# A fused attention and two-layer feed-forward kernel: block sums by accumulating transfers, separate rings for the weight parts, a new order of products and copies

## The chip, the cores and the metric

One core of one Trainium2 chip. The metric is device time in microseconds of the whole kernel; the lower the better. The profile shows one execution on that core. PE is TensorE (matmuls), DVE is VectorE, ACT is ScalarE, POOL is GpSimd, SP is SyncE, whose queue issues most loads. Each engine runs its own instructions in one fixed order.

## The reference

Retention (attention without softmax, with a decay instead) on 4 x 8 heads of 576 tokens of 64, then two feed-forward layers on the 2304 x 512 result:

```
scores = 0.125 * q @ k.T ;  ret = scores * Dmat        # Dmat[i,j] = gamma_h ** (i-j), 0 above the diagonal
x  = (ret @ v), heads side by side                     # 2304 x 512
h  = x @ w_in                                          # 512 -> 2048
g  = (a0 + a1*h + a2*h^2 + a3*h^3) / (1 + |b0|*|h| + |b1|*h^2 + 1e-6)
x  = g @ w_out                                         # 2048 -> 512
g  = s * max(x @ w_in2, 0)^2 + b ;  out = g @ w_out2   # second layer, 2048 wide too
```

All of it is fp32.

## The kernel before

Every product is made of three fp32r matmuls (`three`, line 360): an operand is kept as a rounded high part and a low part (the rest), and high x low, low x high, high x high are added in PSUM. A high part is cast on ACT, a low part is a subtraction on POOL or DVE. Weights come from DRAM as 1 MB tiles `raw` of 64-bit words, one per column tile `kf` (0 to 15 first layer, 16 to 31 second), each with a part of w_in and one of w_out. `w_round` (line 115) rounds them in three DVE steps and one ACT step, `w_split` (line 130) writes high and low parts into one of five slots `w0` to `w4`. `next_load` (line 95) issues the next raw load. Two raw tiles have permanent buffers; tiles 2, 5, 8, ... have a third one that is there only in some stages (`extra_raw`, lines 89 to 97).

*Retention* (lines 151 to 301) runs over 16 pairs of heads; loads go out five pairs ahead on SP. PE, DVE, ACT and POOL orders are pinned to the program order (`keep_in_program_order`). One step of the first three weight cuts stands in each pair from the third on. Line 283 issues raw loads in pairs 3 and 7; the one in pair 7 is tile 2, and the first steps on tile 2 stand in pair 7 as well.

*First layer* (`emit_in`, `rational`, `out1`, lines 385 to 443): 80 units, each a column tile by a block of 512 tokens (or 256, tokens 2048 to 2303). A unit is 12 matmuls into a bank `h`, a chain of 13 ACT, DVE and POOL instructions (`rational`), and 12 matmuls of w_out into four banks `o`, which DVE adds to `acc`. The out-products lag by two or three units. Except where pinned, a planner in the compiler sets the order of instructions within ACT, DVE, POOL and SP from the program order and its own estimate of readiness.

*Second layer.* 16 quads (`quad`, line 666), eight for each pair of 512-token blocks (a pass). A quad takes two column tiles, k = 16 + 2q and k + 1, and makes its four 512 x 128 results with seven half-size products (`PRODUCTS`, line 602, a Winograd scheme) instead of eight. For that it needs sums of token blocks, "1" to "4" (`x_sum`, line 512: four DVE instructions of 1024 elements for each pass, in place in `acc`, then `x_split`), and sums of weights S1 to S4 (`s_sums`, `s_split`). The first quad of each pass works with eight plain products while these are made. `fill` (line 672) sets out-products of the quad before (`out2`; at quad 0 those of the last units) between the products. Results leave a quad by `relu2` (line 612): four ACT instructions and a DVE subtraction. The 256 tail tokens are done in the first pass (`tail_in`, line 656). In pass one every quad rounds and splits the next quad's weights (`cut_first`, `cut_second`), keeps the split parts in DRAM (`w_keep`) and prepares the second pass's token blocks (`x_keep`); the second pass fetches them again (`w_fetch`, `s_fetch`, `x_fetch`), all by POOL's queue.

In a quad the order of the matmuls is product 1, 5, two fills, 6, two fills, 2, fills, 7, fills, 3, two fills, tail, 4, tail. ACT copies the bank of product 1 into hB ahead of product 6:

```
756  nc.scalar.copy(hB, hA)
760  nc.scalar.copy(g5, hG)
763  product(q, 6, hB, False)
790  relu2(("q", q, 1, 0), hB, 512, True)      # last result of a quad, from the same bank hB
```

Of the kernel before, what the change touches and what calls it, by code (L numbers as in the profile page):

```python
# [27 lines left out]
W_BUFS = 5  # L28
W_EARLY = 4
WTMP_BUFS = 1  # L30
RAW_BUFS = 2
# [11 lines left out]
def retention_ffn_kernel(ctx, tc, a, b, s2, b2, w, qkv, maskv, gdec, out):  # L43
# [14 lines left out]
    stg = ctx.enter_context(tc.tile_pool(name="stg", bufs=RAW_BUFS))  # L58
# [23 lines left out]
    w_slots = {}  # L82
    w_both = {}
# [5 lines left out]
    raw_extra = [None]  # L89

    def extra_raw(kf):

        return kf % 3 == 2 and kf < NF

    def next_load(eng=nc.sync, pin=free):
        if w_ahead and not (extra_raw(w_ahead[0]) and raw_extra[0] is None):
            w_load(w_ahead.pop(0), eng, pin)

    def w_slot_tiles(pool, slots):
        for i in slots:  # L100
            w_both[i] = pool.tile([P, 2, 2, NC, P], F32R, name=f"w{i}")
            w_slots[i] = [w_both[i][:, x] for x in range(2)]

    w_slot_tiles(wpool, range(W_EARLY))

    def w_load(kf, eng, pin):
        pool = raw_extra[0] if extra_raw(kf) else stg
        w_raw[kf] = t = pool.tile([P, 2 * DM], I64, tag="raw", name=f"raw{kf}")
        pin(eng.dma_start(out=t, in_=w[kf]))
# [5 lines left out]
    def w_round(kf, pinned=False):  # L115
# [4 lines left out]
        pin = tc.keep_in_program_order if kf < W_FIRST + RAW_BUFS + 1 else free  # L120
# [9 lines left out]
    def w_split(kf, pinned=False):  # L130
        rest = tc.keep_in_program_order if pinned else free
        f = w_words(kf)[1].bitcast(F32)
        wh, wl = w_slots[kf % W_BUFS]
        whf, wlf = (x.rearrange("p w c f -> p (w c f)") for x in (wh, wl))
        for which in range(2):
            w_t[kf, which] = (wh[:, which], wl[:, which])
        rest(nc.scalar.copy(whf, f))  # L137
        nc.gpsimd.tensor_tensor(out=wlf, in0=f, in1=f32(whf), op=ALU.subtract)  # L138
# [12 lines left out]
    def retention(actx):  # L151
# [152 lines left out]
    def ffn(fctx):  # L304
# [11 lines left out]

        rawctx = ExitStack()
        raw_extra[0] = rawctx.enter_context(tc.tile_pool(name="rawx", bufs=1))
        next_load()
# [3 lines left out]
        def raw_to_g():  # L323
            rawctx.close()
            gpx = fctx.enter_context(tc.tile_pool(name="gpx", bufs=1))
            g_free.extend((gpx, i) for i in range(G_BUFS[1] - G_BUFS[0]))
# [16 lines left out]
        def g_tiles(u, n):  # L343
# [5 lines left out]
            pool, i = g_used[u] = g_free.pop(0)  # L349
            whole = [pool.tile([P, 512], F32R, tag=f"{x}{i}", name=f"{x}{number(u)}") for x in ("gh", "gl")]  # L350
# [34 lines left out]
        def emit_in(u):  # L385
# [7 lines left out]
            hps[u] = ps  # L393

        def rational(u):
# [14 lines left out]
            nc.vector.scalar_tensor_tensor(out=tt, in0=r, scalar=-2.0, in1=tt, op0=ALU.add, op1=ALU.mult)  # L410
# [115 lines left out]
        def x_keep(i, c):  # L526
# [9 lines left out]
            if c == 1:  # L536
                for x in NEXT.get(key, ()):
# [19 lines left out]
        def s_sums(q):  # L557
# [5 lines left out]
            nc.vector.tensor_tensor(out=s3, in0=a["11"], in1=a["21"], op=ALU.subtract)  # L563
            nc.vector.tensor_tensor(out=s2, in0=s1, in1=a["11"], op=ALU.subtract)
            nc.vector.tensor_tensor(out=s4, in0=a["12"], in1=s2, op=ALU.subtract)
# [13 lines left out]
        def w_keep(kf):  # L579
            w_spill[kf] = spill.tile([P, 2, 2, NC, P], F32, name=f"ws{kf}")  # L580
            nc.gpsimd.dma_start(out=w_spill[kf], in_=f32(w_both[kf % W_BUFS]))

        def w_fetch(kf):
            nc.gpsimd.dma_start(out=w_both[kf % W_BUFS], in_=w_spill[kf - NF])
            for which in range(2):
                w_t[kf, which] = tuple(x[:, which] for x in w_slots[kf % W_BUFS])

        def s_fetch(q):
            t = stg.tile([P, 2, 2, 512], F32R, tag="raw", name=f"sf{q}")
# [66 lines left out]
        def tail_in(q, i, tag):  # L656
# [4 lines left out]
            for c in range(NC):  # L661
                for x in three(ps, (wh[:, c, :], wl[:, c, :]), (xh[:, c, r], xl[:, c, r]), c == 0, c == NC - 1):
                    pe(x)
            relu2(("q", q, i, 2), ps, n, True)

        def quad(q, fills):
# [42 lines left out]
            def cut_second():  # L709
# [3 lines left out]
                if rounds:  # L713
                    next(rounds[1], None)
                    t = s_sums(q + 1)
                    del w_raw[k + 2]
                    next_load()
                    s_split(q + 1, t)

            if q % (NQ // 2) == 0:  # L720
                fill(4)

                for (i, j), tag, key in zip(((0, 0), (0, 1), (1, 1), (1, 0)), ("hA", "hG", "hB", "hT"), ("1", "3", "2", None)):
# [7 lines left out]
                    if key and first:  # L731
# [182 lines left out]
```

## Time and profile before

| | us |
|---|---|
| median of 3 runs (lowest, highest) | 919.59 (917.74, 922.48) |
| the profiled execution | 917.18 |
| span of the profiled execution | 915.4 |
| mean granted clock of TensorE, share of full speed | 0.983 |

The retention stage ends at about 87 us, the first layer's last out-products at about 520, quad 1 starts at 540, the second pass at about 733, and the last matmul ends at 911. "Idle before" in a row is time in which the engine did nothing just before an instruction, and what ended it. A wait on PE is lost time where PE is the busiest engine; a wait elsewhere matters only through what stands behind it.

### The profile page before, as it was taken

How to read it: one execution, taken by the hardware profiler on the slowest of the kernel's cores; microseconds unless marked ns; L12 is line 12 of the kernel's file. 1: busy time of each engine (PE TensorE's matmuls, PEld its weight loads, DVE VectorE, ACT ScalarE, POOL GpSimd, SP SyncE). 2: the span in 40 equal slices, each digit the busy share in tenths (PEclk: the TensorE clock that was granted, in tenths of full speed). 3: DMA queues.
4: the chain of work that ended last, by engine and by line, in shares of the span. 5: the costliest groups of instructions: out<-in, count | busy, mean ns of one | idle time of the engine just before them, and what ended most of it. 6: DMA issues, size and time to landing. Idle time of an engine off the chain costs nothing.

```text
span 915.4 us, 12746 instructions
## 1 busy us (share of the span) xinstructions
PE 856.1 (94%) x4812; PEld 719.7 (79%) x4812; DVE 627.5 (69%) x923; ACT 602.2 (66%) x1001; POOL 405.5 (44%) x328
## 2 busy tenths in 40 slices
PE   6979999899999799999995869999999999999998
PEld 6869788688888688888883758877778888888886
DVE  4856885997877878768969872877766542444445
ACT  1323997887967778678877468667786556554453
POOL 3855563665764655556679533334433300000000
PEclk9989999999999999999998989999999999999999
DMA  8991210111111100101220633566665964444312
GB/s 331 391 330 38 90 47 1 46 47 47 47 47 47 46 16 32 47 1 47 92 92 18 234 116 113 219 243 226 257 229 197 312 227 150 184 179 155 137 47 93
DMA packets 30030, 119.38 MB, mean 130 GB/s; under 512 B 3600, under 2 KB 4112, under 8 KB 20880
## 3 DMA queue, kind: packets, MB, share of 16 engines
q1 hardware_dynamic: 19168, 65.08, 20.0%
q0 software_dynamic: 10800, 53.48, 15.8%
q8 instruction: 38, 0.62, 0.3%
q14 instruction: 24, 0.20, 0.1%
HBM read 83.42 MB, written 35.13 MB: 130 GB/s over the span
## 4 chain that ended last, share of the span: by engine, by line
PE 48%; DVE 16%; DMA 11%; issue 9%; ACT 8%; POOL 7%; SPq 0%; POOLq 0%; ACTq 0%; DVEq 0%
PE p L363 15%; PE o L363 10%; PE h L363 8%; DMA raw<-in_w_dram 8%; PE hB L363 5%; POOL w L138 4%; PE hA L363 3%; PE hG L363 3%; DVE raw L127 2%; DVE wm L124 2%; DVE h L409 2%; DVE tt L408 2%; DVE acc L425 2%; ACT wm L121 1%; DVE tt L410 1%
## 5 line engine op out<-in xcount | busy, mean ns | idle before, releaser
L363 PE MATMUL p<-w,gh 128*128 128x512 f32 x576 | 189.5, 389 | 0.0
L363 PE MATMUL h<-xh,w 128*128 128x512 f32 (+1 forms) x640 | 185.4, 372 | 0.0
L363 PE MATMUL o<-gh,w 128*128 128x512 f32 (+1 forms) x640 | 184.2, 373 | 0.0
L401 POOL TENSOR_TENSOR tq<-tq,ta 128x512 f32<-128x512 f32 (+1 forms) x80 | 103.5, 1295 | 100.7 <-ACT tq L400 98.8
L363 PEld LDWEIGHTS h<-xh,w 128*128 128x128 f32 x640 | 117.9, 191 | 20.8
L363 PEld LDWEIGHTS o<-gh,w 128*128 128x128 f32 x640 | 117.7, 191 | 20.4
L363 PE MATMUL h<-xl,w 128*128 128x512 f32 (+1 forms) x320 | 120.0, 375 | 12.3 <-DVE tt L410 12.2
L363 PE MATMUL o<-gl,w 128*128 128x512 f32 (+1 forms) x320 | 119.6, 375 | 12.5 <-POOL gl L413 9.4
L363 PEld LDWEIGHTS p<-w,gh 128*128 128x128 f32 x576 | 108.1, 188 | 22.4
L651 DVE TENSOR_TENSOR acc<-acc,p 128x512 f32<-128x512 f32 x126 | 85.9, 684 | 57.6 <-PE p L363 57.0
L413 POOL TENSOR_TENSOR gl<-tt,gh 128x512 fp32r<-128x512 f32 (+1 forms) x80 | 102.4, 1284 | 45.5 <-ACT gh L412 37.8
L363 PE MATMUL p<-w,gl 128*128 128x512 f32 x288 | 112.1, 389 | 0.0
L138 POOL TENSOR_TENSOR w<-raw,w 128x1024 fp32r<-128x1024 f32 x32 | 81.2, 2544 | 63.6 <-ACT w L137 63.4
L363 PEld LDWEIGHTS o<-gl,w 128*128 128x128 f32 x320 | 60.9, 191 | 25.8 <-POOL gl L413 10.7
L363 PEld LDWEIGHTS h<-xl,w 128*128 128x128 f32 x320 | 61.1, 191 | 25.0 <-DVE tt L410 14.7
L403 DVE TENSOR_TENSOR tt<-tt,h 128x512 f32<-128x512 f32 (+1 forms) x80 | 50.3, 629 | 34.0 <-ACT tt L402 33.6
L408 DVE SCALAR_TENSOR_TENSOR tt<-tt,aneg,h 128x512 f32<-128x512 f32 (+1 forms) x80 | 55.1, 688 | 23.4 <-ACT h L407 23.2
L400 ACT ACTIVATE tq<-ta,babs 128x512 f32<-128x512 f32 (+1 forms) x80 | 61.9, 776 | 4.8 <-DVE h L409 4.6
L412 ACT CAST gh<-tt 128x512 fp32r<-128x512 f32 (+1 forms) x80 | 46.1, 577 | 26.6 <-DVE tt L410 19.8
L363 PEld LDWEIGHTS p<-w,gl 128*128 128x128 f32 x288 | 54.0, 188 | 11.5 <-DVE gl L499 0.2
L405 ACT ACTIVATE ta<-tq,lnb 128x512 f32<-128x512 f32 (+1 forms) x80 | 54.5, 684 | 11.6 <-POOL tq L401 11.2
L121 ACT ACTIVATE wm<-raw 128x1024 f32<-128x1024 f32 x32 | 37.2, 1163 | 35.9 <-DMA raw<-in_w_dram 34.1
(121 smaller groups left out, 1657.9 us busy)
## 6 DMA issues: line engine op xcount, KB each, us to landing
raw<-in_w_dram SPq DMA_DIRECT2D x32, 1024.0 KB, 4.9
ws<-w POOLq DMA_DIRECT2D x16, 1024.0 KB, 6.5
w<-ws POOLq DMA_DIRECT2D x16, 1024.0 KB, 7.4
xT<-in_qkv_dram SPq DMA_DIRECT2D x16, 576.0 KB, 8.2
sf<-ss POOLq DMA_DIRECT2D x7, 1024.0 KB, 5.1
xs<-tt POOLq DMA_DIRECT2D x24, 256.0 KB, 3.0
vn<-in_qkv_dram SPq DMA_DIRECT2D x16, 320.0 KB, 8.4
out_dram<-acc SPq DMA_DIRECT2D x18, 256.0 KB, 2.0
```

The source lines that it names most:

```text
L121: pin(nc.scalar.activation(m, hi.bitcast(F32), AF.Copy, scale=2.0 ** -112))
L124: rest(nc.vector.scalar_tensor_tensor(out=t, in0=t, scalar=3, in1=lo, op0=ALU.logical_shift_left, op1=ALU.bitwise_or))
L138: nc.gpsimd.tensor_tensor(out=wlf, in0=f, in1=f32(whf), op=ALU.subtract)
L363: yield nc.tensor.matmul(ps, lhsT=lh, rhs=rh, start=start and x == 0, stop=stop and x == 2, skip_group_check=True)
L400: nc.scalar.activation(tq, ta, AF.Identity, bias=babs[:, 0:1], scale=babs[:, 1:2])
L401: nc.gpsimd.tensor_tensor(out=tq, in0=tq, in1=ta, op=ALU.mult)
L403: nc.vector.tensor_tensor(out=tt, in0=tt, in1=h, op=ALU.mult)
L405: nc.scalar.activation(ta, tq, AF.Ln, bias=lnb, scale=QS)
L408: nc.vector.scalar_tensor_tensor(out=tt, in0=tt, scalar=aneg[:, 0:1], in1=r, op0=ALU.add, op1=ALU.mult)
L412: nc.scalar.copy(gh, tt)
L413: nc.gpsimd.tensor_tensor(out=gl, in0=tt, in1=f32(gh), op=ALU.subtract)
L651: nc.vector.tensor_tensor(out=at, in0=at, in1=ps, op=ALU.add)
```

## The change

Raw tiles get three permanent buffers in rotation (two from tile 15 on; the third then becomes g tiles). The weight slots become ten halves, used as before in the first layer; in the second layer w_in parts rotate over four halves and w_out parts over six, so both tiles of a quad are split in the quad before (`w_split(k + 3)` moves from the start of the next quad into `cut_second`), and both are fetched at the start of the quad before. Transfers to and from DRAM go by halves. Token-block sums become accumulating transfers from POOL's queue, with two blocks of each pass negated on ACT first (the signs of S2 and S3 turn with them). In the first quad of a pass the splits of sums and both cuts are issued behind the last unit's final DVE, ACT and POOL instructions; at quad 0 four fills stand after each product instead of two. In a quad product 3 goes ahead of product 7; the last result (1, 0) and the second tail's are emitted in the next quad, behind its two copies; hB alternates between two banks. Short units of the first layer use all four h banks.

```diff
-RAW_BUFS = 2
+RAW_BUFS = 3
+    def raw_tag(kf):
+        return f"raw{kf % RAW_BUFS if kf < NF - 1 else (kf + 1) % 2}"
     def next_load(eng=nc.sync, pin=free):
-        if w_ahead and not (extra_raw(w_ahead[0]) and raw_extra[0] is None):
+        if w_ahead:
             w_load(w_ahead.pop(0), eng, pin)
...
+    IN_RING = (2, 4, 6, 0)
+    OUT_RING = (3, 5, 7, 8, 9, 1)
+    def w_place(kf):
+        if kf < NF:
+            return 2 * (kf % W_BUFS), 2 * (kf % W_BUFS) + 1
+        return IN_RING[(kf - NF) % len(IN_RING)], OUT_RING[(kf - NF) % len(OUT_RING)]
...
     def w_split(kf, pinned=False):
-        rest(nc.scalar.copy(whf, f))
-        nc.gpsimd.tensor_tensor(out=wlf, in0=f, in1=f32(whf), op=ALU.subtract)
+        for src, dst in todo:
+            rest(nc.scalar.copy(dst[:, 0], src))
+            nc.gpsimd.tensor_tensor(out=dst[:, 1], in0=src, in1=f32(dst[:, 0]), op=ALU.subtract)
...
             if p in (3, 7):
-                raw_extra[0] = sb1
                 next_load(nc.sync, pin)
-                raw_extra[0] = None
...
-            if n < 512 and tag == "hB":
-                bank[0] += 1
-                tag = H_TAGS[bank[0] % H_BUFS]
...
+        def behind_ends():
+            hold = ExitStack()
+            for x in ends:
+                hold.enter_context(tc.issue_after(x.ins))
+            return hold
...
-            nc.scalar.copy(gh, tt)
-            nc.gpsimd.tensor_tensor(out=gl, in0=tt, in1=f32(gh), op=ALU.subtract)
+            ends[:] = [end, nc.scalar.copy(gh, tt),
+                       nc.gpsimd.tensor_tensor(out=gl, in0=tt, in1=f32(gh), op=ALU.subtract)]
...
-        SUMS = {"1": ("12", "11"), "2": ("22", "1"), "3": ("22", "12"), "4": ("21", "2")}
+        SUMS = {"1": "12", "3": "22", "2": "1", "4": "2"}
         def x_sum(pair, key):
-            one, two = (x_at(pair, x) for x in SUMS[key])
-            nc.vector.tensor_tensor(out=x_at(pair, key), in0=one, in1=two, op=ALU.subtract)
+            nc.gpsimd.dma_start(out=x_at(pair, key), in_=x_at(pair, SUMS[key]), accum_op=ALU.add)
+        def x_negate(pair, key):
+            nc.scalar.mul(x_at(pair, key), x_at(pair, key), -1.0)
...
-            if q and first:
-                w_split(k + 1)
-                w_keep(k + 1)
-                del w_raw[k + 1]
-                next_load()
-            if not first:
-                w_fetch(k + 1)
             if NQ // 2 - 1 <= q < NQ - 1:
                 w_fetch(k + 2)
+                w_fetch(k + 3)
...
                     next(rounds[1], None)
+                    w_split(k + 3)
                     t = s_sums(q + 1)
-                    del w_raw[k + 2]
-                    next_load()
+                    for x in (k + 2, k + 3):
+                        del w_raw[x]
+                        next_load()
+                    w_keep(k + 3)
                     s_split(q + 1, t)
...
-                    if key and first:
-                        x_split(0, key)
-                    if (i, j) == (0, 0):
-                        cut_first()
-                    if (i, j) == (1, 1):
-                        cut_second()
-                    fill(2)
+                    with behind_ends():
+                        if key and first:
+                            x_split(0, key)
+                        if (i, j) == (0, 0):
+                            cut_first()
+                        if (i, j) == (1, 1):
+                            cut_second()
+                    fill(4 if first else 2)
...
-            hB = ps_h.tile([P, 512], F32, tag="hB", name=f"hB{q}")
+            hB = ps_h.tile([P, 512], F32, tag=("hT", "hB")[q % 2], name=f"hB{q}")
...
             nc.scalar.copy(g5, hG)
             renew("1")
+            while late:
+                late.pop(0)()
             fill(2)
...
+            product(q, 3, hG, False)
+            relu2(("q", q, 0, 1), hG, 512, True)
+            renew("22")
+            fill(1 + first)
             product(q, 7, hB, False)
...
-            fill(1 + first)
-            product(q, 3, hG, False)
-            relu2(("q", q, 0, 1), hG, 512, True)
-            renew("22")
             cut_second()
...
-            relu2(("q", q, 1, 0), hB, 512, True)
+            late.append(lambda: relu2(("q", q, 1, 0), hB, 512, True))
             renew("12")
             if first:
-                tail_in(q, 1, "o")
+                late.append(tail_in(q, 1, "o", late=True))
...
             if final[0:1024].all() and sums:
-                x_sum(0, sums.pop(0))
+                x = sums.pop(0)
+                if x in ("1", "3"):
+                    x_negate(0, {"1": "11", "3": "22"}[x])
+                x_sum(0, x)
```

## Rows read from the trace of the kernel before

**Rows 1.** The page, part 1: busy us (share of the span) and instructions of each engine.

```profile
PE 856.1 (94%) x4812; PEld 719.7 (79%) x4812; DVE 627.5 (69%) x923; ACT 602.2 (66%) x1001; POOL 405.5 (44%) x328
```

**Rows 2.** Busy time by stretch: us, five engines (instructions), granted clock, DMA share, GB/s.

```profile
48.00:60.00 12.00, 5.14 (x70) 4.96 (x70) 5.09 (x7) 2.23 (x4) 6.46 (x5) 0.72 0.92 369
483.00:516.30 33.30, 20.73 (x73) 14.76 (x72) 33.30 (x44) 21.03 (x34) 27.02 (x17) 0.85 0.19 56
516.30:539.60 23.30, 17.50 (x86) 14.88 (x85) 18.91 (x22) 14.86 (x25) 12.78 (x13) 0.85 0.64 241
705.00:915.00 210.00, 206.53 (x928) 171.19 (x926) 94.16 (x142) 110.41 (x182) 21.52 (x35) 1.00 0.48 168
...
765.00:830.00 65.00, 65.00 (x288) 53.81 (x288) 27.50 (x42) 35.04 (x58) 4.78 (x9) 1.00 0.39 146
```

**Rows 3.** The waits: engine line waited for, us in total, times, longest us.

```profile
POOL w L584 <- PE p L363: 59.7, 8, 24.6
...
PE h L363 <- DVE tt L410: 12.2, 5, 4.8
...
PE hB L363 <- ACT hB L756: 9.4, 6, 2.9
...
PE o L363 <- POOL gl L413: 9.4, 3, 6.3
...
PE pv L229 <- issue: 7.6, 2, 6.9
...
PE ht L363 <- POOL xl L429: 5.8, 1, 5.8
...
PE o L363 <- DVE acc L425: 3.1, 2, 2.2
```

**Rows 4.** The timeline of SP, DVE and PE, 43 to 65 us: start, us, instruction.

```profile
43.34 0.33 SPq L109 DMA_DIRECT2D raw<-in_w_dram  x1
...
54.20 0.70 DVE L122 TENSOR_SCALAR raw<-raw 128x1024 uint32<-128x1024 uint32 x1 [7.25 <-DMA raw<-in_w_dram]
...
47.82 0.99 PE L241 MATMUL pv<-xT,spre 64*64 64x128 f32 x16
...
60.22 0.99 PE L241 MATMUL pv<-xT,spre 64*64 64x128 f32 x16
...
64.51 0.99 PE L241 MATMUL pv<-xT,spre 64*64 64x128 f32 x16
```

**Rows 5.** Groups of DVE, ACT and POOL, 483.0 to 516.3: busy us, mean ns | idle before.

```profile
L514 DVE TENSOR_TENSOR acc<-acc 128x1024 f32<-128x1024 f32 x4 | 9.2, 2291 | 0.0
...
L499 DVE TENSOR_TENSOR xl<-acc,xh 128x1024 fp32r<-128x1024 f32 x2 | 3.5, 1760 | 0.0
...
L499 DVE TENSOR_TENSOR xl<-tt,xh 128x512 fp32r<-128x512 f32 x2 | 2.4, 1213 | 0.0
...
L518 ACT CAST xh<-acc 128x1024 fp32r<-128x1024 f32 x3 | 3.2, 1054 | 0.5 <-DVE acc L514 0.5
...
L138 POOL TENSOR_TENSOR w<-raw,w 128x1024 fp32r<-128x1024 f32 x2 | 5.7, 2858 | 0.6 <-ACT w L137 0.5
...
L499 POOL TENSOR_TENSOR xl<-acc,xh 128x1024 fp32r<-128x1024 f32 x1 | 2.4, 2368 | 0.0
...
L535 POOL DMA_DIRECT2D xs<-tt x1 | 0.6, 600 | 0.9 <-ACT tt L532 0.9
```

**Rows 6.** DMA issues: KB each, median us from issue to landing.

```profile
ss<-xh SPq DMA_DIRECT2D x7, 512.0 KB, 3.0
...
xh<-xs POOLq DMA_DIRECT2D x6, 512.0 KB, 8.1
```

**Rows 7.** The timeline of PE: first matmul of quad 1 and of quad 7.

```profile
539.58 0.40 PE L363 MATMUL hA<-xl,w 128*128 128x512 f32 x1
...
707.03 0.40 PE L363 MATMUL hA<-xl,w 128*128 128x512 f32 x1
```

More of the change, by code (lines that the diff above doesn't have):

```diff
@@ L132, in w_split @@
         f = w_words(kf)[1].bitcast(F32)
[L133 to L136, printed above, removed]
-        rest(nc.scalar.copy(whf, f))
-        nc.gpsimd.tensor_tensor(out=wlf, in0=f, in1=f32(whf), op=ALU.subtract)
+        w_views(kf)
+        i, j = w_place(kf)
+        if kf < NF:
+            t, n = w_halves[i]
+            todo = [(f.rearrange("p (w x) -> p w x", w=2), t[:, :, n:n + 2, :])]
+        else:
+            todo = [(f[:, DM * x:DM * (x + 1)], w_half(y)) for x, y in enumerate((i, j))]
+        for src, dst in todo:
+            rest(nc.scalar.copy(dst[:, 0], src))
+            nc.gpsimd.tensor_tensor(out=dst[:, 1], in0=src, in1=f32(dst[:, 0]), op=ALU.subtract)
     def w_cut(kf, pinned=False):
@@ L323, in raw_to_g @@
         def raw_to_g():
-            rawctx.close()
-            gpx = fctx.enter_context(tc.tile_pool(name="gpx", bufs=1))
-            g_free.extend((gpx, i) for i in range(G_BUFS[1] - G_BUFS[0]))
+            x = stg.tile([P, 2, G_BUFS[1] - G_BUFS[0], 512], F32R, tag="raw2", name="gx")
+            g_free.extend((x, i) for i in range(G_BUFS[1] - G_BUFS[0]))
         def region(t0, n):
@@ L348, in g_tiles @@
                 g_done(next(iter(g_used)))
-            pool, i = g_used[u] = g_free.pop(0)
-            whole = [pool.tile([P, 512], F32R, tag=f"{x}{i}", name=f"{x}{number(u)}") for x in ("gh", "gl")]
+            place, i = g_used[u] = g_free.pop(0)
+            if place is gp:
+                whole = [gp.tile([P, 512], F32R, tag=f"{x}{i}", name=f"{x}{number(u)}") for x in ("gh", "gl")]
+            else:
+                whole = [place[:, x, i, :] for x in range(2)]
             if type(u) is tuple and u[2:] == (0, 2):
@@ L393, in emit_in @@
             hps[u] = ps
+        ends = []
+        def behind_ends():
[3 more added lines that the diff above has]
+            return hold
         def rational(u):
@@ L579, in w_keep @@
         def w_keep(kf):
-            w_spill[kf] = spill.tile([P, 2, 2, NC, P], F32, name=f"ws{kf}")
-            nc.gpsimd.dma_start(out=w_spill[kf], in_=f32(w_both[kf % W_BUFS]))
+            for x, i in enumerate(w_place(kf)):
+                w_spill[kf, x] = spill.tile([P, 2, DM], F32, name=f"ws{2 * kf + x}")
+                nc.gpsimd.dma_start(out=w_spill[kf, x], in_=f32(w_half(i)))
         def w_fetch(kf):
-            nc.gpsimd.dma_start(out=w_both[kf % W_BUFS], in_=w_spill[kf - NF])
-            for which in range(2):
-                w_t[kf, which] = tuple(x[:, which] for x in w_slots[kf % W_BUFS])
+            w_views(kf)
+            for x, i in enumerate(w_place(kf)):
+                nc.gpsimd.dma_start(out=w_half(i), in_=w_spill[kf - NF, x])
         def s_fetch(q):
-            t = stg.tile([P, 2, 2, 512], F32R, tag="raw", name=f"sf{q}")
+            t = stg.tile([P, 2, 2, 512], F32R, tag=f"raw{q % 2}", name=f"sf{q}")
             nc.gpsimd.dma_start(out=t, in_=s_spill[q - NF // 2])
@@ L654, in out2, with tail_in @@
                 nc.sync.dma_start(out=out[t0 + e * P:t0 + (e + 1) * P, :], in_=at)
-        def tail_in(q, i, tag):
+        late = []
+        def tail_in(q, i, tag, late=False):
             r = slice(2048, NT)
@@ L663, in tail_in @@
                     pe(x)
+            if late:
+                return lambda: relu2(("q", q, i, 2), ps, n, True)
             relu2(("q", q, i, 2), ps, n, True)
@@ L761, in quad @@
             renew("1")
+            while late:
+                late.pop(0)()
             fill(2)
@@ L801, in ffn @@
         sums = ["1", "3", "2", "4"]
+        raw_gone = []
         first_rounds = None
@@ L806, in ffn @@
             emit_cuts(u)
-            if not items and not cuts and rawctx is not None:
+            if not items and not cuts and not raw_gone:
                 raw_to_g()
-                rawctx = None
+                raw_gone.append(u)
             for x in outs_at[u]:
@@ L832, in ffn @@
             rest = outs_of(q)
+        while late:
+            late.pop(0)()
         for x in rest:
```

41 lines of the change are left out of this document (21 added, 20 removed).

## The prediction

> **What bounds the kernel now.** I read the page's first part, then the waits, then busy time by stretch. PE is busy 94% of the span, DVE 69%, ACT 66%, POOL 44% [rows 1], so only time in which PE stands still, or runs at the lower clock, can be won. In the last pass PE is never kept waiting: 288 matmuls of 512 columns in 65.00 us, 0.226 us each [rows 2], at full clock. Its idle time is elsewhere, in five kinds of wait of a microsecond and more [rows 3]: 7.6 us in the attention stage ("issue"), 12.2 us for a bank of h, 12.5 us for gl and for evictions of o, 5.8 us for xl of the tail, 9.4 us for the copy that fills hB. The stretches show the same [rows 2]: from 48 to 60 us PE works 5.14 of 12 at a clock of 0.72; from 483.0 to 516.3 DVE is busy all 33.30 us while PE has 20.73; from 516.3 to 539.6 PE has 17.50 of 23.30. Both of the latter stand at a clock of 0.85: part of them ran at 1.2 GHz instead of 2.4, after PE had stood still. From 705 us PE has 206.53 of 210. The change can win in the first, third and fourth of these and in the hB waits, and nothing after 705.
>
> **Third raw buffer from the start: 7 us.** Before, raw tile 2 had a place only at pair 7, so its load goes out at 43.34. DVE's first step on it is next in DVE's pinned order; it starts at 54.20 after 7.25 us of waiting [rows 4]. Everything behind it on DVE and ACT waits too, and with it PE: one pair takes from 47.82 to 60.22, 12.40 us, the next 64.51 - 60.22 = 4.29 [rows 4], a loss of 8.1. With its own buffer the load is issued when cut 0 ends, in pair 5, at least two pairs (8.6 us) earlier, more than the wait. SP's queue gains nothing in all; the megabyte only moves ahead of other loads, whose tiles are fetched five pairs ahead. Bounds: 0 (the wait passes to vn or xT) to 8.1; I take 7, as the wait is covered but attention loads arrive a little later. Tile 5 is loaded earlier too, after the last attention load: nothing.
>
> **Sums by transfers, and work put behind the last results: 11 us in 483 to 516.** DVE is the bound there. It loses four sums, 9.2 us, two splits of them, 3.5, and two splits of weight sums, 2.4 [rows 5]: 33.3 - 15.1 = 18.2. ACT loses three casts of 1.05 and gains two negations, priced by the same row as 1024 elements from and to SBUF [rows 5]: 21.0 - 3.2 + 2.1 = 19.9. POOL loses two subtractions of a cut, 5.7, and a split, 2.4, and gains four issues of 0.6 [rows 5]: 27.0 - 8.1 + 2.4 = 21.3. The longest is POOL's 21.3; the last units are a chain through all three engines, so I take 22.3 and a gain of 11. Bounds: 0 (latency fills the place of work) to 12.
>
> **What was held back comes next: 4.3 us in 516 to 540.** Two cuts, two weight-sum splits and three splits are now issued behind the last unit's results, so they fall here; the next quad's cuts, which are here now, move on by a quad. I take DVE's load as unchanged, 18.9 us [rows 2]. PE needs 48 full matmuls and 36 of half length: 48 x 0.226 + 36 x 0.113 = 14.9. DVE is the longer one: 19.0 instead of 23.3. The four out-products ahead of the second and third product of quad 0, in place of two, end the tail's evictions earlier; the 5.8 us wait for xl [rows 3] is inside this sum, and what is late next is the S operand of quad 1's fifth product. Bounds: 0 to 23.3 - 14.9 = 8.4.
>
> **Price of the sums: 3.6 us back.** Each sum reads what the one before wrote, or writes what it reads; so each waits for the last to land, and the wait stands in POOL's queue, with the units' squares and gl behind it. The trace has no accumulating transfer. Nearest are 512 KB stores of 3.0 us and 512 KB loads of 8.1 us to landing [rows 6]; a sum reads both sides, so I take twice the store, 6. The sums are emitted one per unit; a unit is 24 matmuls, 5.4 us. Three waits: 3 x (6 + 0.6 - 5.4) = 3.6. Ends: 0 (3.0 us) and 3 x 3.3 = 9.9 (8.1 us). Below nothing is excluded: the sums' DVE time has already been credited. For the second half the sums are spread over six quads; POOL is busy little there and a quad lies between a sum and its use: nothing, unless a sum takes most of a quad. The Trainium skill ("DMA: Bandwidth & Descriptors", section "Anatomy of one DMA — SWDGE (gpsimd) path") fits a transfer from POOL as 2.0 us plus bytes over 436 GB/s, an estimate of 3.2 us for 512 KB; by it nothing would be held and the sum below would be 3.6 us better. The trace agrees with it for the stores only; loads of that size took 8.1 [rows 6].
>
> **Late results and the other bank of hB: 8.5 us.** Six quads wait for ACT's copy into hB, 9.4 us in all [rows 3]; the copy stood behind the last result of the quad before (four ACT instructions) and the tail's. These now follow it. Quad 1 starts at 539.58 and quad 7 at 707.03 [rows 7]: 27.9 us each. A quad is 102 full matmuls and 24 half ones: 23.05 + 2.7 = 25.8, so 2.1 x 6 = 12.6 us is the most. Cut, splits and the tail that stays still lie ahead of the copy, so I take 8.5. Bounds 0 to 12.6. Late next are the (1,0) results, wanted only after two groups of fills and two products, 36 matmuls or 8.1 us later.
>
> **Edits taken as nothing.** Third product ahead of the seventh: hG was ready long before, the sum from hB now has two fills and no product to cover it (2.7 us for 0.7 of DVE); if that cover is gone, 0.5 us a quad. In the very last quad the (1,1) result is wanted sooner: 0 to 0.5. Separate rings: fetches wait for nothing at the start of a quad, where POOL waits 59.7 us for PE now [rows 3], but PE has no wait on them. Halving splits and transfers adds 32 issues of 0.6 on POOL in 400 us, under idle POOL; in pieces of 2 KB the transfers could be slower, covered by a quad. On SP both raw loads of a quad now go out together at its end, ahead of the stores of the weight sums; the first is wanted some 8 us into the next quad (36 matmuls), and if it is late ACT stands in front of it, inside the 12.6. The h banks turn by four also for short units; the other 10 us of h waits may move by 4 either way.
>
> **Sum.** 7 + 11 + 4.3 - 3.6 + 8.5 = 27.2. The profiled execution took 917.18 us, span 915.4; 917.2 - 27.2 = 890.0. The median of the runs, 919.59, is 2.4 above it, so **892**.
>
> **Rivals.**
> *Better, 0.15:* all bounds at the good end, 8.1 + 12 + 8.4 + 12.6 = 41.1, 878 with the 2.4. For: ACT and POOL are far from full. Against: the copy still shares ACT's queue.
> *The held-back work returns, 0.19:* quad 1 waits for what was moved, so the second stretch gains nothing and the first half: 27.2 - 4.3 - 5.5 = 17.4, 905. For: DVE at 18.9 of 23.3 already.
> *A part does not do what it says, 0.07:* the planner still puts ACT's copy behind a cut, or the raw load goes out no earlier: 27.2 - 8 = 19, 901.
> *No change, 0.06:* sums that take 12 us to land hold POOL 3 x 7.2 = 21.6; with a quarter of the 30.8 lost as in the second rival, 23.1 - 21.6 = 1.5 remains: 915.7, with the 2.4 918. For and against as in the next.
> *Slower, 0.05:* the chain of sums decides. Gains without the hold are 30.8; three waits eat them when a sum lands after 30.8 / 3 + 5.4 - 0.6 = 15.1 us. At 18 us it is 3 x 12.8 = 38.4 - 30.8, 7.6 slower: 927. For: POOL's queue does stand in waits for transfers [rows 3]. Against: the slower kind of 512 KB transfer took 8.1 [rows 6]. The Trainium skill ("DMA: Bandwidth & Descriptors", the same section) says that a wait for a semaphore stands on the issuing sequencer and never on the transfer engines; the trace agrees, with POOL's 59.7 us ahead of fetches [rows 3].
>
> **How the numbers follow.** The forecast has 0.48. To leave out no more than 2 in 10 the range takes in the better case, 878, and the returned work with the hold at its far end, 905 + 9.9 - 3.6 = 911; no change and slower stay outside. A measurement here can tell 0.5% (4.6 us) from no change. Faster by more: 0.48 + 0.15 + 0.19 + 0.07 = 0.89; same 0.06; slower 0.05.
>
> **What would show it.** Right: no DVE wait of 7 us near 47 us and pairs of 4.3 us; no L514 on DVE; the stretch from the last h matmul to quad 1 under 40 us; no PE wait on the hB copy above 0.5 us. Wrong: gl or squares starting late on POOL behind an accumulating transfer; hG of quad 1 waiting for the S operand; DVE or ACT waiting for raw tiles in the quads; waits of PE after 705.

## The result, and the profile after

Four runs of each kernel side by side: 919.64 us before, **896.55 us** after (892.61 to 899.40), a ratio of 0.974 with a 95% interval of 0.969 to 0.980. The profiled execution of the kernel after took 898.97 us, span 897.2. It lies 2.4 us above its median, and that of before 2.5 us below its own, so the two traces show 18.2 of the 23.1 us.

The page of the kernel after, first part (busy us, share of the span, instructions; answers to [rows 1]):

```profile
PE 857.3 (96%) x4812; PEld 721.8 (80%) x4812; DVE 628.6 (70%) x915; ACT 607.4 (68%) x1021; POOL 437.6 (49%) x384
```

The shares of busy time hardly move; the stretches of time tell more. The kernel after: the first layer from the first to the last h matmul, from there to quad 0, quad 0, quads 1, 2, 3 to 7, and the second pass (columns as in [rows 2]):

```profile
87.00:475.00 388.00, 384.69 (x1859) 324.13 (x1857) 315.66 (x483) 321.52 (x531) 241.53 (x185) 1.00 0.13 46
475.00:491.00 16.00, 13.05 (x49) 9.61 (x49) 14.04 (x21) 11.27 (x18) 11.46 (x11) 0.89 0.52 98
491.00:511.40 20.40, 18.08 (x87) 14.87 (x86) 20.30 (x21) 12.97 (x24) 15.62 (x14) 0.92 0.28 102
511.40:547.30 35.90, 29.67 (x128) 23.91 (x127) 22.95 (x28) 28.31 (x51) 17.84 (x19) 0.90 0.78 273
547.30:582.80 35.50, 29.09 (x128) 23.25 (x127) 27.55 (x35) 22.94 (x42) 15.49 (x17) 0.90 0.56 207
582.80:720.40 137.60, 136.46 (x656) 114.68 (x655) 96.55 (x137) 99.24 (x178) 63.88 (x75) 1.00 0.80 260
```

The same stretches of the kernel before, where [rows 2] do not have them: the first layer, quads 1, 2, 3 to 7.

```profile
87.00:490.00 403.00, 388.03 (x1860) 325.34 (x1858) 322.90 (x487) 321.31 (x529) 240.53 (x178) 0.99 0.13 45
...
539.60:568.80 29.20, 26.27 (x128) 21.88 (x127) 8.59 (x12) 22.16 (x40) 5.32 (x5) 1.00 0.23 87
568.80:595.90 27.10, 26.41 (x129) 22.02 (x128) 22.03 (x32) 20.21 (x36) 10.95 (x11) 1.00 0.61 232
595.90:738.50 142.60, 136.81 (x656) 114.25 (x655) 97.94 (x146) 98.44 (x172) 52.71 (x55) 1.00 0.70 251
```

Two of these are surprises. The first layer is 15 us shorter, with 3.3 us of idle PE where there were 15.0. And quads 1 and 2 are 15 us *longer*, at a granted clock of 0.90: PE stood still there, and part of the stretch ran at 1.2 GHz instead of 2.4. What PE waited for in the kernel after, in the first layer, up to quad 1, in quads 1 and 2, and in quads 3 to 7 (columns as in [rows 3]):

```profile
PE h L378 <- DVE tt L431: 3.2, 2, 1.9
...
PE o L378 <- POOL gx L434: 2.5, 1, 2.5
PE o L378 <- DVE acc L446: 2.2, 1, 2.2
...
PE p L378 <- DVE gl L520: 4.4, 2, 2.2
PE hG L378 <- DVE gx L520: 3.2, 1, 3.2
PE hB L378 <- DVE ta L814: 3.0, 1, 3.0
PE p L378 <- ACT gh L654: 2.0, 1, 2.0
...
PE hB L378 <- DVE ta L814: 0.8, 1, 0.8
```

The waits of h and of hB in [rows 3] are nearly gone, 12.2 to 3.2 and 9.4 to none on the copy. In quads 1 and 2 there are 12.6 us of new ones. The timeline of DVE in quad 1 has their origin:

```profile
537.62 0.70 DVE L137 TENSOR_SCALAR raw<-raw 128x1024 uint32<-128x1024 uint32 x1 [5.13 <-DMA raw<-in_w_dram]
...
541.32 0.70 DVE L137 TENSOR_SCALAR raw<-raw 128x1024 uint32<-128x1024 uint32 x1 [1.38 <-DMA raw<-in_w_dram]
...
543.07 0.68 DVE L520 TENSOR_TENSOR gx<-hA,gx 128x512 fp32r<-128x512 f32 x1
543.67 0.68 DVE L814 TENSOR_TENSOR ta<-hB,tq 128x512 f32<-128x512 f32 x1
```

L137 is the first step on a raw tile. DVE stood 5.13 and 1.38 us for two tiles, with the results of product 2 (`gx`) and the second sum of hB (`ta`) behind it in its fixed order; PE waited 3.0 us for that sum. In quads 1 and 2 DVE stands 15.8 us for raw tiles in all, and 5.8 in the kernel before: such waits are not new, but more of them now have a result behind them.

All stages, from the first matmuls of each in the timeline of PE (us; "to quad 1" is from the last row of h to quad 1; "pass 2" ends at the start of PE's last row). A row can merge several matmuls. So the first layer may read 0.1 us short, and pass 2 reads 0.5 us short where it has 172.04: the last matmul itself starts 172.5 us into the pass in the kernel after and 172.6 before.

| kernel | first h | first layer | to quad 1 | quads 1, 2 | quads 3 to 7 | pass 2 | median |
|---|---|---|---|---|---|---|---|
| before | 87.15 | 403.18 | 49.25 | 56.28 | 142.68 | 172.60 | 919.64 |
| after | 86.38 | 388.46 | 36.58 | 71.40 | 137.61 | 172.04 | 896.55 |
| e1, third raw load in order | 80.80 | 388.44 | 36.58 | 69.96 | 136.89 | 172.04 | 891.86 |
| e2, second split moved back | 85.18 | 388.43 | 36.52 | 71.15 | 138.13 | 172.04 | 897.69 |
| e3, short units skip hB | 87.08 | 397.74 | 37.83 | 73.34 | 142.04 | 172.04 | 916.03 |
| e4, sums on DVE | 85.19 | 390.24 | 41.98 | 64.83 | 140.82 | 172.04 | 899.02 |
| e5, roundings behind results | 84.70 | 388.43 | 36.57 | 54.24 | 158.90 | 181.66 | 910.96 |
| e6, product 7 ahead of 3 | 85.58 | 388.48 | 36.58 | 68.18 | 140.79 | 172.59 | 899.76 |
| e7, no late results | 84.54 | 388.37 | 34.99 | 71.29 | 137.83 | 172.04 | 896.17 |
| e8, before, banks of four | 87.02 | 388.84 | 48.94 | 52.96 | 142.13 | 172.59 | 902.43 |
| e9, roundings behind first sum | 80.65 | 388.31 | 36.53 | 52.74 | 146.12 | 177.56 | 887.81 |
| e10, that in quads 1, 2 only | 82.61 | 388.23 | 36.48 | 52.09 | 159.57 | 172.04 | 896.27 |
| e11, copies not held | 87.16 | 392.44 | 48.75 | 60.76 | 141.13 | 172.03 | 907.50 |
| e12, e9 with two edits | 82.99 | 388.18 | 36.56 | 52.10 | 147.02 | 181.41 | 894.01 |

A stage that an edit leaves alone repeats within 0.1 us (the first layer of e1, e2, e5 to e7) except the first column, which moves by some 2 us between executions. So a stage tells more than the medians, whose intervals are 0.2 to 0.6% to either side.

### The profile page after: what moved, and what is told of

Same layout as the page of the kernel before. It is cut to its first block, busy times and chain, and to the rows that moved or that the text cites. A ratio compares the mean times of both kernels' runs of the same rounds, so it can differ in the third digit from the quotient of the medians.

```text
span 897.2 us, 12864 instructions
## 1 busy us (share of the span) xinstructions
PE 857.3 (96%) x4812; PEld 721.8 (80%) x4812; DVE 628.6 (70%) x915; ACT 607.4 (68%) x1021; POOL 437.6 (49%) x384
## 5 line engine op out<-in xcount | busy, mean ns | idle before, releaser
L378 PE MATMUL o<-gh,w 128*128 128x512 f32 (+1 forms) x592 | 166.7, 367 | 0.0
L378 PE MATMUL p<-w,gh 128*128 128x512 f32 x336 | 123.4, 392 | 2.0 <-ACT gh L654 2.0
L378 PEld LDWEIGHTS o<-gh,w 128*128 128x128 f32 x592 | 107.0, 189 | 18.1
L378 PE MATMUL o<-gl,w 128*128 128x512 f32 (+1 forms) x296 | 108.8, 369 | 2.8 <-DVE acc L446 2.2
L434 POOL TENSOR_TENSOR gl<-tt,gh 128x512 fp32r<-128x512 f32 (+1 forms) x74 | 92.3, 1253 | 37.7 <-ACT gh L433 27.1
L157 POOL TENSOR_TENSOR w<-raw,w 128x512 fp32r<-128x512 f32 (+1 forms) x48 | 87.8, 1838 | 35.3 <-ACT w L156 27.8
L378 PE MATMUL p<-w,gx 128*128 128x512 f32 x360 | 100.5, 396 | 0.0
L378 PEld LDWEIGHTS p<-w,gx 128*128 128x128 f32 x360 | 69.3, 193 | 14.7
L378 PEld LDWEIGHTS p<-w,gh 128*128 128x128 f32 x336 | 63.5, 189 | 15.8 <-ACT gh L654 2.7
L613 POOL DMA_DIRECT2D w<-ws x32 | 22.4, 703 | 100.2 <-PE hA L378 50.9
L378 PE MATMUL p<-w,gl 128*128 128x512 f32 x168 | 66.1, 394 | 4.4 <-DVE gl L520 4.4
L378 PEld LDWEIGHTS o<-gl,w 128*128 128x128 f32 x296 | 55.7, 189 | 13.5 <-DVE acc L446 2.6
```

The lines of the kernel that those rows point to most:

```text
L157: nc.gpsimd.tensor_tensor(out=dst[:, 1], in0=src, in1=f32(dst[:, 0]), op=ALU.subtract)
L378: yield nc.tensor.matmul(ps, lhsT=lh, rhs=rh, start=start and x == 0, stop=stop and x == 2, skip_group_check=True)
L613: nc.gpsimd.dma_start(out=w_half(i), in_=w_spill[kf - NF, x])
```

## The experiments

**The banks of h** (e3 undoes the edit in the kernel after; e8 makes it alone in the kernel before).

```diff
 def h_tile(u, n):
     tag = H_TAGS[bank[0] % H_BUFS]
-    if n < 512 and tag == "hB":
-        bank[0] += 1
-        tag = H_TAGS[bank[0] % H_BUFS]
     bank[0] += 1
```

> One edit to the kernel after: units of 256 tokens skip bank hB again, as before. Theory: taking the banks in an even turn of four is what made the first layer shorter (first to last h product 388.5 us in the kernel after, 403.2 before; the waits of h for the rational's last steps at 173.9, 304.1 and 431.1 us are gone): then the first layer takes 398 to 404 us again and the time rises by 9 to 15 us, to 906 to 911 us. Rival: the raw buffers' ring or the place of the cuts did it; then the first layer stays at 387 to 391 us and the time at 895 to 899 us.

> One edit to the kernel before: units of 256 tokens no longer skip bank hB; nothing else of the change. Theory: the skip cost the first layer most of what the change gained there (putting it back made that layer 9.3 us longer); then first to last h product fall from 403.2 us to 390 to 396 and the time by 7 to 13 us, to 907 to 913 us. Rival: it counts only with the new ring of raw buffers and cuts; then the first layer stays above 400 us and the time at 917 to 921 us.

e3: 916.03, 19.5 us above the kernel after; only 9.3 of them are in the first layer, and quads 1 to 7 lose 6.4 in all, with the order that the planner then makes. e8: 902.43, a ratio of 0.980 (0.977 to 0.984): **three deleted lines alone give 18.7 us**, 14.3 of them in the first layer and 3.3 in quads 1 and 2. Both theories had the direction, and both times moved by more than their prices. The first layer of e8, its stretch and its waits for h:

```profile
87.00:476.00 389.00, 383.95 (x1862) 323.39 (x1860) 322.07 (x487) 321.62 (x529) 239.66 (x178) 1.00 0.13 47
```

```profile
PE h L363 <- DVE tt L407: 3.9, 3, 1.9
```

From 87 to 475 us the kernel before waits 10.3 us in 4 such waits, e3 9.6 in 5:

```profile
PE h L378 <- DVE tt L434: 9.6, 5, 2.9
```

PE's idle time in the first layer falls from 15.0 us in the kernel before to 5.1 in e8, and its busy time from 388.0 to 384.0. Behind its two longest waits PE works on at a lower clock. The stretch behind the longest one (4.75 us, to 304.06) in the kernel before, at 0.76:

```profile
304.00:311.00 7.00, 6.94 (x23) 5.57 (x24) 5.97 (x11) 4.87 (x8) 2.95 (x3) 0.76 0.00 1
```

How does a skipped bank lead to these waits? By the program order a unit that skips, and the two behind it, get banks that were last used three units ago instead of four. But no wait of PE above 0.4 us falls on these units. PE and DVE of the kernel before, around the first group of short units (L410 is the last read of a bank of h):

```profile
145.41 0.39 PE L363 MATMUL h<-xl,w 128*128 128x512 f32 x1
...
154.86 0.28 PE L363 MATMUL h<-xl,w 128*128 128x256 f32 x1
...
173.86 0.50 PE L363 MATMUL h<-xl,w 128*128 128x512 f32 x1 [2.51 <-DVE tt L410]
```

```profile
173.13 0.68 DVE L410 SCALAR_TENSOR_TENSOR tt<-h,tt 128x512 f32<-128x512 f32 x1
175.46 0.68 DVE L410 SCALAR_TENSOR_TENSOR tt<-h,tt 128x512 f32<-128x512 f32 x1
```

The wait ends with the last read of four units earlier (173.8). The banks of the three units between are read until 176.1, 184.4 and 189.2, so no other bank stood free. What differs is PE's order of units. The short units come in groups of five. In the two kernels with the skip the planner puts one full unit ahead of the last two or three of them (here at 145.41, so the fifth starts at 154.86). In e8 and the kernel after the five follow each other, and in e8 the fifth starts at 149.42. Of the three long waits in the kernel before, those that end at 304.06 and 431.08 then go, and the first one shrinks from 2.5 to 1.9 us. Whether the order does this or the banks themselves, no run separates.

**The third raw load** (e1, on the kernel after).

```diff
 def w_cut(kf, pinned=False):
     ...
-    next_load()
+    next_load(pin=tc.keep_in_program_order if kf == 0 else free)
```

> One edit to the kernel after: the third raw weight load (the one that the first cut releases) keeps its place in the written order of SP's queue, so that it is issued behind the attention loads of pair 8 and not at 14 us among those of the first pairs. Theory: in the kernel after the early transfer pushes the attention loads back (pair 4 to pair 5 took 9.2 us there, 4.0 before), and this ate the gain of the third buffer; then the first h product starts at 79 to 82 us (86.4 in the kernel after, 87.2 before), everything behind it is unchanged, and the time falls by 4 to 7 us, to 890 to 893 us. Rival: the pairs are held by the rounding steps on VectorE, whenever the load comes; then the first h product stays at 85.5 to 87 us and the time at 896 to 898 us.

891.86, the first h matmul at 80.80: both as the theory had them. In the kernel after, SP, POOL and PE show what the early load cost; in e1 the same load goes out at 34.78:

```profile
14.16 0.33 SPq L124 DMA_DIRECT2D raw<-in_w_dram  x1
```

```profile
34.78 0.37 SPq L124 DMA_DIRECT2D raw<-in_w_dram  x1
```

```profile
32.09 1.26 POOL L219 TENSOR_TENSOR vn<-vn,mv 128x640 f32<-128x640 f32 x1 [6.63 <-DMA vn<-in_qkv_dram]
```

```profile
33.41 0.89 PE L248 MATMUL pv<-vn,kn 128*64 128x128 f32 x16 [3.51 <-POOL vn L219]
```

A load with a free buffer and no place in the pinned order was issued 29 us earlier than before (43.34, [rows 4]), ahead of attention loads that are needed first. With the load in its place PE's wait on vn is gone, DVE does not wait for a raw tile there either, and the third buffer gives 6.4 us (4.2 to 6.5 in the four kernels with this edit).

**From the last h matmul to quad 1** (e4: DVE subtractions in place of the transfers and negations; e11: nothing held behind the last results; both on the kernel after).

```diff
 def x_sum(pair, key):
-    nc.gpsimd.dma_start(out=x_at(pair, key), in_=x_at(pair, SUMS[key]), accum_op=ALU.add)
+    one, two, op = ...
+    nc.vector.tensor_tensor(out=x_at(pair, key), in0=x_at(pair, one), in1=x_at(pair, two), op=op)
```
```diff
 def behind_ends():
     hold = ExitStack()
-    for x in ends:
-        hold.enter_context(tc.issue_after(x.ins))
     return hold
```

> One part of the kernel after undone: the sums of token blocks are made by VectorE again (subtractions, so that the negations on ScalarE go too), everything else stays, the held-back copies and the fills of four among it. Theory: the sums by transfers took some 9 us of work from VectorE between the last h product and quad 1, and half of it was on the path; then that stretch goes from 36.6 us to 41 to 46 us and the time rises by 4 to 9 us, to 900 to 906 us. Rival: what shortened the stretch is that copies wait behind the last results and that each product has four fills; then the stretch stays at 36 to 38 us and the time at 895 to 899 us.

> One part of the kernel after undone: copies and weight work of the first quad are not held behind the last results of the first layer; sums by transfers and four fills a product stay. From last h product to quad 1 the kernel before takes 49.3 us, after 36.6, after with sums on VectorE 42.0, so the other parts are worth 7.3 us here. Theory: holding the copies back is most of it; then the stretch goes to 40 to 45 us and the time rises by 3 to 8 us, to 899 to 905 us. Rival: the four fills and the planner's order do it; then the stretch stays at 35.5 to 38 us and the time at 895 to 899 us.

The stretch takes 49.25 us before and 36.58 after; without the transfers 41.98, without the hold 48.75. So beside the hold the transfers shorten it by 5.4 us, and beside the transfers the hold shortens it by 12.2. With transfers but no hold (e11) it is hardly shorter than before: the transfers are worth little without the hold, as far as these runs go; none has both undone. Without the hold PE waits again for the last units (waits of e11, 474 to 512 us):

```profile
PE o L378 <- DVE acc L444: 6.5, 2, 5.1
PE o L378 <- POOL gx L432: 5.9, 1, 5.9
PE h L378 <- DVE tt L429: 3.9, 1, 3.9
```

e4's stretch came as its theory had it; its time rose by 2.5 us only, less than priced, since quads 1 and 2 gave 6.6 back. e11's theory had the cause, but its stretch and its time (907.50) lie above their ranges. Its first layer is 4.0 us longer too, and quads 1 and 2 give 10.6 back, so part of what the hold gains before quad 1 it costs in those quads. How long each of the first four sums takes to land, and what stood for it, in the kernel after (tile `acc`, 460 to 500 us):

```profile
L535 POOL DMA_DIRECT2D acc<-acc x4: 862/916/1232, 468.1 to 486.3; - x4
...
  POOL acc L535: 2.6, 1
...
DMA to landing us min/median/max: 4.5/4.5/4.9
```

**Late results** (e7, on the kernel after).

```diff
-    late.append(lambda: relu2(("q", q, 1, 0), hB, 512, True))
+    relu2(("q", q, 1, 0), hB, 512, True)
...
-        late.append(tail_in(q, 1, "o", late=True))
+        tail_in(q, 1, "o")
```

> One part of the kernel after undone: the squares of a quad's last product and of its second piece of the tail are issued at once and not behind the next quad's first two products. Theory: late results were given 8.5 us in the prediction with the bank of hB; then quads 3 to 7 rise from 137.6 us to 140 to 144 and the time by 2 to 7 us, to 898 to 904 us. Rival: the bank in turn (hB and hT) alone removed the hB wait, and the place of the squares is nothing; then quads 3 to 7 stay within 1.5 us and the time at 895 to 898 us.

The rival came true: 896.17, quads 3 to 7 at 137.83. The waits on the hB copy stay away without late results. What is left to have removed them is that hB alternates between two banks; that was not undone by itself.

**Quads 1 and 2.** e2 moves the second split back to the next quad, with the raw loads apart; e6 undoes the order of products 7 and 3.

```diff
+    if q and first:
+        w_split(k + 1); w_keep(k + 1); del w_raw[k + 1]; next_load()
...
-            w_split(k + 3)
             t = s_sums(q + 1)
-            for x in (k + 2, k + 3):
-                del w_raw[x]
-                next_load()
-            w_keep(k + 3)
+            del w_raw[k + 2]
+            next_load()
```
```diff
+    product(q, 7, hB, False)
+    ...
     product(q, 3, hG, False)
     ...
-    product(q, 7, hB, False)
-    ...
```

> One edit to the kernel after: the split of a quad's second weight tile goes back to the start of the next quad, as before, so that the two raw loads of a quad go out half a quad apart and not together at its end. Theory: quads 1 and 2 take 71.4 us in the kernel after (56.3 before) because VectorE and ScalarE stand for raw words that were asked for too late (3.3 and 5.1 us on VectorE), with the sum of hB and the squares of the products queued behind; then quads 1 and 2 take 56 to 60 us together, their granted clock is back at 1.00, and the time falls by 10 to 15 us, to 882 to 887 us. Rival: it is the order of the products (the sum from hB has only two fills to cover it); then quads 1 and 2 still take 67 us or more and the time is 893 to 900 us.

> One edit to the kernel after: the seventh product stands ahead of the third again. Theory (waits for raw words are the cause in quads 1 and 2): only the hB waits of 3.0 and 0.8 us behind the second sum go, quads 1 and 2 stay at 66 to 71 us, and the time falls by 1 to 4 us, to 892 to 896 us. Rival (the swap of the products is what quads 1 and 2 lost by): quads 1 and 2 fall to 56 to 62 us and the time to 882 to 888 us. That the swap is worth something to quads 3 to 7: they rise by 2 us or more from 137.6.

e2 told nothing apart: the planner still issued both loads together, 19.4 us into quad 1 (20.2 in the kernel after), and quads 1 and 2 took 71.15 us. SP of the kernel after, SP and DVE of e2 (quad 1 starts at 511.4 and 510.1):

```profile
531.61 0.80 SPq L124 DMA_DIRECT2D raw<-in_w_dram  x2
```

```profile
529.56 0.80 SPq L124 DMA_DIRECT2D raw<-in_w_dram  x2
```

```profile
536.12 0.70 DVE L137 TENSOR_SCALAR raw<-raw 128x1024 uint32<-128x1024 uint32 x1 [5.69 <-DMA raw<-in_w_dram]
```

e6 is worth nothing in time: quads 1 and 2 fall by 3.2 us, quads 3 to 7 rise by 3.2. Its median is 3.2 above that of the kernel after, with overlapping intervals. So quads 1 and 2 came as its theory had them (66 to 71 us), but the time (892 to 896) did not fall. To move the roundings themselves, e5 ties them to results:

```diff
-    cut_first()
+    with tc.issue_after(on_act.ins), tc.issue_after(on_dve.ins):   # copy of hG, first sum
+        cut_first()
...
-    cut_second()
+    with tc.issue_after(on_act.ins), tc.issue_after(on_dve.ins):   # cast of result (0, 1), second sum
+        cut_second()
```

> The kernel after with one addition: in each quad the rounding of the next quad's first weight tile stands on VectorE behind that quad's first sum of hB and hG and on ScalarE behind the copy of hG, and the rounding of the second tile behind the second sum of hB and behind the copy of the second product's results; TensorE's order stays as it is. (In the second run of this study the split moved in the program text only; the written order of the engines came out the same, and quads 1 and 2 took 71.2 us.) Theory: quads 1 and 2 are long because these roundings are issued up to a quad ahead and stand for raw words while results wait behind them; then quads 1 and 2 take 55 to 61 us together (71.4 in the kernel after), quads 3 to 7 stay at 136 to 139, and the time is 881 to 888 us. Rival: the weights' sums come later by as much and the fifth product waits for them, or the transfers' throughput (DMA share about 1.0 at 536 to 548 us) is the bound; then quads 1 and 2 stay above 66 us and the time is 891 to 899 us.

(The cast of the second tie is that of result (0, 1), which product 3 makes; the text above calls it the second product's.) Theory and first rival both came true, in different quads, and the time of 910.96 lies above both ranges. Stretches of e5 (quads 1 and 2, quads 3 to 7), and its waits from 563 to 735 us:

```profile
509.70:563.90 54.20, 52.59 (x254) 43.91 (x253) 36.00 (x51) 46.00 (x83) 19.75 (x23) 1.00 0.60 214
563.90:722.80 158.90, 146.63 (x656) 120.05 (x655) 113.19 (x149) 106.05 (x186) 76.62 (x88) 0.95 0.76 252
```

```profile
PE hG L378 <- DVE xl L520: 10.7, 5, 2.6
PE hs L378 <- DMA xl<-xs: 7.3, 1, 7.3
```

Quads 1 and 2 fall from 71.4 to 54.2 us at a clock of 1.00. TensorE works the same tiles in the same order there, and DVE no longer stands for a raw tile: **DVE and ACT standing for raw tiles, with results behind, is what quads 1 and 2 lost by**. But from quad 3 on the weights' sums (`xl`) are late for the fifth product, and the second pass waits for its token blocks. e9 ties both cuts to the first sum (and keeps e1's edit); e10 does so in quads 1 and 2 alone; e12 is e9 with quad 6's second cut tied as in e5, and e7's edit.

```diff
     cut_second()   # e9: behind the copy of hG and the first sum, as cut_first
     # e10: both "if q < 3"
     # e12: for q == 6 behind the cast of result (0, 1) and the second sum
```

> The kernel after with the third raw load in its written place (as in the first run) and, in every quad, both roundings of the next quad's weight tiles behind that quad's first sum of hB and hG on VectorE and behind the copy of hG on ScalarE: the second tile's no longer as late as in the fifth run, where quads 1 and 2 fell to 54.2 us but quads 3 to 7 rose to 158.9 us because the fifth product waited some 2.3 us in each for the weights' sums. Theory: the sums come some 7 us earlier in a quad than there, so that quads 1 and 2 take 53 to 57 us, quads 3 to 7 137 to 142, the second pass 172 to 173, and the time is 872 to 879 us. Rival: the sums are late again (the fifth product waits, quads 3 to 7 above 148 us): 884 to 895 us.

> The ninth run's kernel with the roundings held behind the first sum in quads 1 and 2 alone. Theory: the planner, free again from quad 3 on, issues quad 3's roundings ahead of that quad's first sum, and they stand for raw words there: the wait moves to quad 3 (30 us or more) and the time is 875 to 883 us, above the ninth run's. Rival: from quad 3 on there is work enough on VectorE in front of them, as in the kernel after: quads 3 to 7 stay at 136 to 138 us and the time is 870 to 876 us.

> The ninth run's kernel with two more edits: in quad 6 alone the rounding of the second weight tile stands behind that quad's second sum of hB (in the ninth run quad 6 took 33.6 us: VectorE stood 3.8 us for a raw tile that took 13.5 us to land, with the evacuations of the fills behind it), and the late results of the seventh run are undone (that run's stretch from last h product to quad 1 was 35.0 us against 36.6). Theory: quad 6 falls to 27 to 30 us, quad 7 and the second pass stay at about 209 us together, and the time is 879 to 885 us (887.8 in the ninth run). Rival: the weights' sums of quad 7 come later by what the rounding is put off, and quad 7 and the copies that the second pass fetches are later by as much: quads 6 and 7 and the second pass keep their sum of 243 us, and the time is 885 to 890 us.

e9, **887.81** (ratio 0.965, 0.963 to 0.966), is the fastest kernel of the study, yet its time lies above its theory and in its rival's range: quads 1 to 5 take 133.2 us, but quad 6 takes 33.6, and the second pass 5.5 more than in the kernel after, where it waits for token blocks as in e5 (2.9 and 2.0 us). SP and DVE of e9 there:

```profile
642.72 0.51 SPq L124 DMA_DIRECT2D raw<-in_w_dram  x1
```

```profile
651.15 0.69 DVE L797 TENSOR_TENSOR hG<-hB,tq 128x512 f32<-128x512 f32 x1
...
656.21 0.69 DVE L137 TENSOR_SCALAR raw<-raw 128x1024 uint32<-128x1024 uint32 x1 [3.77 <-DMA raw<-in_w_dram]
```

DVE's first step on the second raw tile comes 13.5 us after its issue. e10 (896.27): the waits move on as its theory has it, to quads 3 to 6, and cost more than its price. e12 (894.01, above both its ranges): quad 6 falls to 28.1, but quad 7 rises to 37.7 and the second pass by 3.9, the rival with 4 us more on top (243.2 to 247.2 for the three); another 2.3 us are in the first column. Without late results e7's stretch to quad 1 was 1.6 us shorter (34.99), and e12's is not (36.56). e12's waits, 640 to 735 us:

```profile
PE hs L378 <- DMA xl<-xs: 6.9, 1, 6.9
PE hG L378 <- DVE xl L520: 4.9, 2, 3.1
```

In these versions whatever is put behind the results is late for what comes next. In e9's quad 6 two raw loads and two stores of weight sums go out within 2 us, and the DMA engines are busy 0.92 of 640 to 657 us. That this crowding makes the tile late is a reading of the trace and was not tested. A version without any of these waits was not found.

## Why the prediction was right, point by point

The time (892 for 896.55) and the direction were right, and three of the steps were not: their errors cancel, so that the forecast came this close is luck. By the profiled executions, 27.2 us were forecast and 18.2 came (0.8 + 12.7 - 10.0 + 14.7 by the items below).

- **Third raw buffer, 7: got 0.8**, less than the 2 us by which this column moves. The wait of 7.25 us [rows 4] did go. What failed is "the megabyte only moves ahead of other loads, whose tiles are fetched five pairs ahead": an unpinned load with a free buffer went out at 14.16 us, as early as the planner liked and not when cut 0 ends, and vn came late. It is the bound 0 of that term, "the wait passes to vn or xT". In its place in the order it gives 6.4 (e1).
- **483 to 540, 11 + 4.3 - 3.6 = 11.7: got 12.7.** Right as a sum, and by its mechanism: the work had to go from DVE *and* behind the last results (e4, e11). Each of the first four sums landed in 4.5 to 4.9 us, under the 6 taken, and POOL stood once, 2.6 us, not three times 1.2. The Trainium skill's line for transfers from POOL ("DMA: Bandwidth & Descriptors", section "Anatomy of one DMA — SWDGE (gpsimd) path") gave an estimate of 3.2; the trace has 1.3 to 1.7 more. The 3.0 us stores that the prediction set beside it go by SP's queue [rows 6] and not by POOL's, so they do not bear it out. Beside the other transfers of the quads, the four sums of the second half took 4.7 to 12.2 us to land; POOL stood 1.6 us for one of them, so "nothing" holds there as far as POOL's waits go.
- **Late results and the other bank, 8.5: got -10.0 in quads 1 to 7.** The 9.4 us of waits on the hB copy went as said, and quads 3 to 7 gained 5.1; late results had no part in it (e7). The step that failed is among the "edits taken as nothing": that a late raw tile would be "inside the 12.6". It was taken for ACT and the hB copy, within one quad. In fact DVE and ACT took the roundings up to a quad ahead, DVE stood 3.3, 1.3, 5.1, 1.4 and 4.7 us for raw tiles, and the sums and results of products were held behind them: -15.1 in quads 1 and 2 (e5). It is one of the signs that the prediction named for being wrong, "DVE or ACT waiting for raw tiles in the quads".
- **Third product ahead of the seventh, nothing:** right in total, by two halves of 3.2 (e6), not the 0.5 a quad; the "two fills and no product to cover" the second sum of hB cost its 3.0 us where DVE was held.
- **h banks of four, nothing, "may move by 4 either way": got 14.7** in the first layer, the largest term of all (e8 has 14.3 of it alone, e3 loses 9.3 of it). The step gave no reason for its 4. It left out that the rule on banks also sets the planner's order of units, and that the clock is lower behind the longest waits (0.76 from 304 to 311 us).
- **Rivals.** "The held-back work returns" came in another form, in quads 1 and 2, by raw tiles, not at quad 1's start. The chain of sums never decided. Two figures of the rivals do not come out: with 17.4 us gained the time is 902 and not 905, so the far end of the range would be 908.5 and not 911; and sums of 18 us would hold 3 x 13.2, not 3 x 12.8, which makes 928. Neither touches the forecast.

## What to carry to other kernels

Price the smallest edit with the same care as the largest: a rule on which buffer is next also goes into the order that a planner makes, so compare the orders before and after, and not the waits alone. Where a planner orders the queues, a freed buffer or an operand with slack means issue *earlier*, and an engine with one fixed order then stands for the load with urgent work behind it; look for what it will be ahead of, and tie it to a result of the stage where it belongs. Undo parts one at a time, and read each by stage: the medians of e4, e6 and e7 are within 0.4% of the kernel after, while a stage moved by up to 6.6 us.

## What the runs showed of the hardware

DVE's additions of weight words took 0.41 us each at 575 us and 2.74 and 3.26 us at 548 us, while POOL was in subtractions. DVE and POOL of the kernel after:

```profile
548.45 2.74 DVE L588 TENSOR_TENSOR tt<-raw 128x256 f32<-128x256 f32 x1
551.11 3.26 DVE L589 TENSOR_TENSOR tt<-raw,raw 128x256 f32<-128x256 f32 x1
...
575.63 0.41 DVE L588 TENSOR_TENSOR tt<-raw 128x256 f32<-128x256 f32 x1
```

```profile
548.19 2.70 POOL L157 TENSOR_TENSOR w<-raw,w 128x512 fp32r<-128x512 f32 x2
...
551.36 1.50 POOL L157 TENSOR_TENSOR w<-raw,w 128x512 fp32r<-128x512 f32 x1
552.62 1.46 POOL L520 TENSOR_TENSOR tt<-acc,tt 128x512 fp32r<-128x512 f32 x1
```

The Trainium skill ("SBUF — State Buffer", section "Who interferes with whom") states that a DVE instruction with two SBUF inputs contends with a GpSimd instruction that reads SBUF; by that rule the two would go one after the other, and the trace agrees: DVE's two end at 551.2 and 554.4, just behind POOL's ends at 550.9 and 554.1. No run here took that POOL work away, so how much of quad 2 it cost stays open. A raw tile of 1 MB took 13.4 us to land in e9's quad 6 (5.8 in the median of the kernel after), with another raw load issued 1.1 us ahead of it and two 512 KB stores within 1 us.
